# Reloading the second MLP's weights into whichever slot is freed next, with four staging slots and another rhythm of weight conversion

## The chip, the cores and the metric

One core of a Trainium2 chip runs the whole kernel in one launch. The metric is device time in microseconds (us). The kernel before took 1173.22 us, the median of three runs from 1171.08 to 1174.09. Its engines are TensorE (PE, with its weight loads as PEld), VectorE (DVE), ScalarE (ACT), GpSimd (POOL) and SyncE (SP), which issues every DMA of the part looked at here.

## The reference

Attention with a learned bias is followed by two MLPs; the change lies in the second one.

```python
x = attention(q, k, v, bias)              # 2304 tokens x 512
h = x @ w_in; x = (h - tanh(h)) @ w_out   # first MLP, 2048 wide
gate = 1 / (1 + exp(-(x @ w_gate)))       # second MLP, 1536 wide
out = (gate * (x @ w_val)) @ w_out2
```

All data are float32. Each matrix operand is split into a high and a low part (fp32r), and each product is three matmuls: high by high, low by high, high by low.

## The kernel before

**Units and slots.** The second MLP works on 18 units, listed in `PAIRS`. A unit is one pair of 384-token blocks (768 tokens) with one pair of 128-wide feature tiles, `fp`, of six. The list goes through five segments (`SEGS`): tokens 0 with `fp` 0 to 2, tokens 1 with `fp` 0 to 2, tokens 2 with all six, then tokens 0 and 1 again with `fp` 3 to 5. Units are numbered from 0 here. Tokens change after units 2, 5, 11 and 14, and this is what "a change of tokens" means below. A unit takes 14 slots (`slot2`), numbered 0 to 13: seven combined products `j` (a Strassen-like scheme with seven products in place of eight) for the gate half (`m` = 0, slots 0 to 6) and the same seven for the value half (`m` = 1, slots 7 to 13). Over the whole stage slot s is slot s mod 14 of unit s // 14.

**A slot.** It issues six matmuls of a product into one of two PSUM banks (`product`, L866), then, in twelve of the 14 slots, three matmuls of the second projection of the unit before (`down`, L882; slots 12 and 13 have none). Then the bank is emptied (`evacuate`: ACT at L924 and L931, DVE at L927, L933, L937, L941). The two banks alternate, so the product of a slot waits until the product two slots earlier has been emptied. POOL multiplies by the gate (L952) and makes low parts (L916), ACT makes high parts (L701).

**Weights.** Each unit needs nine weight tiles of 512 KB: seven for the products, in the order of their slots, and two for the second projection. They are converted once, stored in DRAM (`wsc`, L609), and reloaded for each unit that uses them (`feed`, L815), 162 reloads in all. Before, the reload with number k always takes place k mod 13 of a ring of 13 SBUF slots, and so waits until the reload k - 13 has been used for the last time (`spent`). Three other slots are staging for newly converted tiles on their way to DRAM (`W.stages`).

**Conversion.** Some weights are still converted while the second MLP runs (`convert`, advanced by one step after a slot). A weight item takes DVE operations at L547, L548, L549 and L545, ACT casts at L556, POOL operations at L554 (low part) and L604 (mix) and an ACT scan at L533. It runs through seven steps before, so one item in seven slots, from slot 8 of the stage to about slot 123. No step is taken in slots for which `slot2` returns true.

**Change of tokens.** In the last unit of a segment, in slots 7 to 13, `x_next` makes the next tokens' operands: for each product ACT casts two tiles (L797), POOL and DVE subtract one each (L797), and DVE does two more operations at L792. In the slots around it the old token results leave (L893 and L896 on DVE and ACT, L898 on SP) and new tokens are read (L775).

The order of the work on each engine is the order in which the code is written; there is no scheduler. Each engine's queue is taken in order, SP's too.

Of the kernel before, what the change touches and what calls it, by code (L numbers as in the profile page):

```python
# [436 lines left out]
GROUPS2 = len(PRODUCTS)  # L437
SLOTS2 = 2 * GROUPS2
PER_FP = GROUPS2 + 2
X_SLOTS, T_SLOTS, RING_SLOTS = tuple(range(14)), (14, 15), 13  # L440
STAGE1 = (0, 1, 2, 3)
X0_AT = N1 - 4
SEGS = ((0, 0, 3), (1, 0, 3), (2, 0, NFP), (0, 3, NFP), (1, 3, NFP))
# [191 lines left out]
def mlps(tc, st, xr, x0, W, xs, x2s, y2s, out, consts):  # L635
# [137 lines left out]
    def src_load(tau, kt):  # L773
        sx[kt] = x0.tile([128, TP], F32, name="xt")
        nc.sync.dma_start(sx[kt], x2s[128 * kt:128 * kt + 128, TP * tau:TP * tau + TP])  # L775
# [26 lines left out]
          N1: ([], [(4, 0), (4, 1)])}  # L802

    loads = [(u, i) for u in range(len(PAIRS)) for i in range(PER_FP)]
    ring, held, issued, spent = [], {}, [0], set()

    def feed():
        while issued[0] < len(loads):
            k = issued[0]
            u, i = loads[k]  # L810
            fp = PAIRS[u][2]
            if (fp, i) not in W.stored or k >= len(ring) and (k < RING_SLOTS or loads[k - RING_SLOTS] not in spent):
                return
            w = W.slot(ring[k % RING_SLOTS])
            nc.sync.dma_start(w.bitcast(F32).rearrange("p a c -> p (a c)"), W.wsc[fp][i])  # L815
            held[loads[k]] = w
            issued[0] += 1

    freed = {W.of[k, f]: LAST[1, f // NPR] + (3 if k == "o" else 1) for k in "io" for f in range(FA, NF1)}
    RING = sorted(freed, key=lambda i: (freed[i], i))  # L820

    def convert():
        while W.made <= W.n:
            highs, lows, mixes, conv = W.step()
            for f in conv[:2]:
                f()
                yield
            for f in highs + lows:
                f()
            for f in conv[2:]:  # L830
                f()
                yield
            for f in mixes:
                f()
            yield
            W.scan()
            yield
            yield
    banks, sums, posts, downs, res = [], [], {}, [], {}

    def at(s, f):
        posts.setdefault(s, []).append(f)
# [9 lines left out]
    def mat(s):  # L852
        g, j = divmod(s, GROUPS2)
        u, m = divmod(g, 2)
        return u, m, j

    def product(s):
        u, m, j = mat(s)
        w = held[u, j]
        p = banks[s % 2]  # L860
        fresh = j in (0, 1, 4)
        for kp in range(2):
            x = xw[PRODUCTS[j], kp]
            for i, (a, c) in enumerate(P3):
                o = 256 * m + 128 * kp
                T.matmul(p, w[:, a, o:o + 128], x[:, c], start=(fresh and kp == 0 and i == 0),  # L866
                         stop=(kp == 1 and i == 2), skip_group_check=True)
        if m:
            spent.add((u, j))

    def down():
        if not downs:
            return
        u, f, t, d, last = downs.pop(0)
        g, tau, fp, at_, n = PAIRS[u]
        h, l = res[u, f, t]
        w = held[u, GROUPS2 + f]
        begin = at_ == 0 and f == t
        end = at_ == n - 1 and f != t
        c = slice(128 * d, 128 * d + 128)  # L880
        for i, (x, a) in enumerate(((h, 0), (h, 1), (l, 0))):
            T.matmul(sums[3 * t + d], x[:, c], w[:, a], start=(begin and i == 0), stop=(end and i == 2))  # L882
        if last:
            spent.add((u, GROUPS2 + f))
        if end:
            return lambda: leave(g, t, d)

    def leave(g, t, d):
        tau, lo, hi = SEGS[g]
        r = TB * t + 128 * d  # L890
        if lo:
            o = kept.pop((t, d))
            V.tensor_add(o, sums[3 * t + d], o)  # L893
        else:
            o = ob.tile([128, DM], F32, name="o")
            (V.tensor_copy if d % 2 else A.copy)(o, sums[3 * t + d])  # L896
        r += TP * tau
        nc.sync.dma_start((out if hi == NFP else y2s)[r:r + 128, :], o)  # L898
# [66 lines left out]
    def slot2(s):  # L965
        u, m, j = mat(s)
        g, tau, fp, p, n = PAIRS[u]
        W.tick()
        feed()
        product(s)  # L970
        left = down()
        evacuate(s)
        if left:
            at(s + 1, left)
        for f in posts.pop(s, []):
            f()
        if g + 1 < len(SEGS):
            if p == n - 3 and m == 1 and j < 4:
                src_load(SEGS[g + 1][0], j)
            if p == n - 2 and j < 3:  # L980
                combine(m, j)
            if p == n - 1 and m == 1:
                x_next(j)
        if SEGS[g][1] and p == n - 1 and m == 0 and j < 6:
            bring(tau, j)
        return g + 1 < len(SEGS) and (p == n - 2 and j < 3 or p == n - 1 and m == 1 and j == 2)

    def x_next(j):
        k = PRODUCTS[j]
        for kp in range(2):  # L990
            for f in x_make(k, kp, (G, V)[kp]):
                f()
        if k == 2:
            for kp in range(2):
                combine(kp, 3)
# [4 lines left out]
    s = 0  # L1000
    for n in range(N1 + 3):
        if n < N1:
            W.tick()
        if n == 2:
            acc = st.enter_context(tc.tile_pool(name="ps_a", bufs=4, space=PSUM, side="right"))
        acts = second(n - 1) if ok(n - 1) else []
        acts[2:2] = [lambda m=m: fourth(m) for m in due(n, 1)]
        vecs = [f for m in due(n, 0) for f in third(m)]
        low, mixes, conv = [], [], []
        if 2 <= n < N1 and n not in X0_STEPS and not any(ends(m) and block(m)[2] for m in due(n - 1, 2)):  # L1010
            h, low, mixes, conv = W.step()
            acts += h
        if n in X0:
            conv = [lambda p=p: combine(*p) for p in X0[n][0]]
        for f in acts:
            f()
        zip_run(vecs, conv)
        if n in X0:
            for p in X0[n][1]:
                h, l = x_make(*p, G)  # L1020
                h()
                low.append(l)
        if n == N1:
            only1.close()
            ev = st.enter_context(tc.tile_pool(name="p3e", bufs=6))
            upst.close()
            one = st.enter_context(tc.tile_pool(name="ps_w", bufs=1, space=PSUM))
            banks = [one.tile([128, 512], F32, name=f"sum{i}")[:, 0:TB] for i in range(2)]
            W.raw2 = st.enter_context(tc.tile_pool(name="wr2", bufs=2))
            ob2 = st.enter_context(tc.tile_pool(name="p2o2", bufs=2))  # L1030
            W.stages = RING[RING_SLOTS:]
            W.lag = 4
        for _ in range({N1: 2, N1 + 1: 5}.get(n, 0)):
            slot2(s)
            s += 1
        for m in due(n - 1, 2):
            if ends(m):
                sixth(m)
        if ok(n):
            for _ in first(n):  # L1040
                if n < 2:
                    yield
        for m in due(n, 2):
            fifth(m)
        for l in low + mixes:
            l()
        if n < N1:
            W.scan()
        if ok(n) and ok(n + 1):
            for ahead in range(1, 5):  # L1050
                if ok(n + ahead) and block(n + ahead - 1) != block(n + ahead):
                    for f, lead in ((x_split, 3), (x_load, 4)):
                        for kt in range(4):
                            if lead - kt // 2 == ahead:
                                f(block(n + ahead), kt)
        if ok(n - 1) and block(n - 1)[2] == 1 and ends(n - 1):
            partial(n - 1)
        if n == X0_AT:
            for kt in range(4):
                src_load(0, kt)  # L1060
        if n >= X0_AT:
            ring += [i for i in RING if freed[i] == n or n == X0_AT and freed[i] < n]
            ring[RING_SLOTS:] = []
            feed()
        yield
    b = odd.tile([128, 2, 512], F32, name="up")
    sums = [b[:, i] for i in range(2)] + [acc.tile([128, 512], F32, name="acc") for _ in range(4)]
    conv = convert()
    while s < SLOTS2 * len(PAIRS):
        full = slot2(s)  # L1070
        if s == SLOTS2 // 2:
            for _ in range(2):
                W.load()
        if s > SLOTS2 // 2 and not full:
            next(conv, None)
        s += 1
        yield
# [124 lines left out]
```

## Time and profile before

| | |
|---|---|
| median of three runs | 1173.22 us (1171.08 to 1174.09) |
| profiled execution, its own time | 1171.4 us |
| span of its instructions | 1169.6 us |
| before the part of the second MLP alone, 0 to 738.67 us | PE busy 706.82 us |
| second MLP alone, 738.67 to 1169.60 us | PE busy 416.04 of 430.93 us, DVE 205.52, ACT 136.82, POOL 214.81 |
| weight reloads `w<-wsc` | 162 of 512 KB, median 7.4 us from issue to landing |

A share of busy time is an average over the stretch that it is taken from. An idle time in brackets in a timeline row is the time in which the engine stood still just before the row's first instruction, with what ended it.

### The profile page before, as it was taken

To read this page: it belongs to the slowest core of one execution; us is meant where nothing else is said; L and a number is where in the kernel's file an instruction comes from. 1 tells how busy PE (TensorE), PEld (TensorE's weight loads), DVE (VectorE), ACT (ScalarE), POOL (GpSimd) and SP (SyncE) were. 2 spreads that over 40 slices of the span, in tenths; PEclk is the share of its full clock that TensorE was granted. 3 is DMA by queue.
4 is the path that set the end of the run, shared out by engine and by line. 5 is a ranking of instruction groups with operands and counts; after the bars stand their busy time and mean duration, and the time that the engine had idled before them with its cause. 6 is when DMAs were issued, how large, how long until landed. Compare 5 with 4: busy or idle time off the path is not lost.

```text
span 1169.6 us, 19994 instructions
## 1 busy us (share of the span) xinstructions
PE 1122.9 (96%) x6968; PEld 978.5 (84%) x6968; DVE 829.3 (71%) x1443; ACT 672.6 (58%) x1341; POOL 667.9 (57%) x602
## 2 busy tenths in 40 slices
PE   5679999999999999999999999999989999999998
PEld 2246776677679999999999999998879999989987
DVE  8878888888659889898889887556566523533523
ACT  7877878787657676677766667234244222423321
POOL 1047777778635555496858667455676543523532
PEclk9889999999999999999999999999999999999999
DMA  6754636373213333355665667876987875685563
GB/s 202 258 177 129 195 112 199 121 210 108 86 48 103 105 107 114 127 195 182 213 207 176 214 238 266 292 274 243 353 313 286 310 294 210 247 295 219 220 255 138
DMA packets 107636, 235.09 MB, mean 201 GB/s; under 512 B 12688, under 2 KB 52880, under 8 KB 107536
## 3 DMA queue, kind: packets, MB, share of 16 engines
q1 hardware_dynamic: 107536, 233.82, 57.7%
q8 instruction: 56, 0.92, 0.3%
q14 instruction: 44, 0.36, 0.1%
HBM read 172.55 MB, written 61.22 MB: 200 GB/s over the span
## 4 chain that ended last, share of the span: by engine, by line
PE 86%; DMA 3%; ACT 3%; DVE 2%; issue 2%; POOL 2%; SPq 0%; DVEq 0%; ACTq 0%; POOLq 0%
PE sum L866 20%; PE acc L727 16%; PE up L663 16%; PE acc L882 8%; PE sc L227 6%; PE pv L319 6%; PE pt L269 6%; PE up L882 4%; DMA w<-wsc 2%; PE bt L75 1%; PE pv L316 1%; ACT e L86 1%; ACT y L62 1%; DMA bsc<-e 1%; POOL w L554 1%
## 5 line engine op out<-in xcount | busy, mean ns | idle before, releaser
L866 PE MATMUL sum<-w,w 128*128 128x384 f32 x1512 | 304.2, 340 | 10.4 <-DMA w<-wsc 3.3
L866 PEld LDWEIGHTS sum<-w,w 128*128 128x128 f32 x1512 | 270.2, 188 | 35.5 <-issue 5.8
L663 PE MATMUL up<-xt,w 128*128 128x384 f32 x1152 | 208.4, 335 | 0.3 <-DVE t L697 0.3
L663 PEld LDWEIGHTS up<-xt,w 128*128 128x128 f32 x1152 | 200.1, 188 | 2.9 <-issue 2.2
L727 PE MATMUL acc<-gh,w 128*128 128x384 f32 x768 | 195.5, 335 | 0.1
L259 POOL TENSOR_SCALAR n<-n,rec 128x576 f32<-128x576 f32 x144 | 120.8, 853 | 83.4 <-ACT n L248 41.1
L554 POOL TENSOR_TENSOR w<-wu,w 128x512 fp32r<-128x512 f32 x86 | 128.4, 1504 | 64.5 <-ACT w L556 64.5
L708 POOL TENSOR_TENSOR gl<-t,gh 128x384 fp32r<-128x384 f32 x96 | 103.8, 1103 | 91.2 <-issue 51.1
L727 PEld LDWEIGHTS acc<-gh,w 128*128 128x128 f32 x768 | 138.3, 188 | 1.2 <-DVE o L746 1.1
L727 PE MATMUL acc<-gl,w 128*128 128x384 f32 x384 | 128.3, 334 | 0.0
L241 DVE CUSTOM_DVE_ANT_0 n<-sc,bias 128x576 f32<-128x576 f32 x144 | 103.7, 753 | 29.7 <-PE sc L227 25.8
L916 POOL TENSOR_TENSOR gl<-e,gh 128x384 fp32r<-128x384 f32 x54 | 58.7, 1092 | 101.7 <-ACT gh L701 101.7
L248 ACT ACTIVATE n<-n,mn 128x576 f32<-128x576 f32 x144 | 111.4, 783 | 8.7 <-DVE mn L241 8.6
L701 ACT CAST gh<-t 128x384 fp32r<-128x384 f32 x114 | 57.7, 516 | 60.4 <-POOL t L952 59.3
L692 ACT ACTIVATE z<-z,c 128x768 f32<-128x768 f32 x48 | 45.2, 941 | 78.9 <-DVE up L691 78.8
L882 PE MATMUL acc<-w,gh 128*128 128x512 f32 x288 | 90.1, 393 | 0.0
L693 DVE TENSOR_TENSOR t<-up,t 128x768 f32<-128x768 f32 x48 | 46.0, 958 | 53.4 <-ACT t L680 52.7
L269 PE MATMUL pt<-ident,n 128*128 128x128 f32 x576 | 80.4, 281 | 1.4 <-ACT at L299 1.3
L654 POOL TENSOR_TENSOR xt<-xm,xt 128x384 fp32r<-128x384 f32 x48 | 49.3, 1047 | 53.9 <-ACT xt L653 50.5
L319 PE MATMUL pv<-at,vs 128*64 128x320 f32 (+1 forms) x512 | 79.3, 421 | 0.0
L941 DVE TENSOR_TENSOR e<-sum,e 128x384 f32<-128x384 f32 x70 | 38.8, 555 | 52.0 <-PE sum L866 52.0
L269 PEld LDWEIGHTS pt<-ident,n 128*128 128x128 f32 x576 | 63.5, 141 | 12.6 <-issue 11.4
(111 smaller groups left out, 2145.5 us busy)
## 6 DMA issues: line engine op xcount, KB each, us to landing
w<-wsc SPq DMA_DIRECT2D x162, 512.0 KB, 7.4
wsc<-w SPq DMA_DIRECT2D x54, 512.0 KB, 5.6
wraw<-in_wo SPq DMA_DIRECT2D x28, 512.0 KB, 4.4
bsc<-e SPq DMA_DIRECT2D x36, 295.5 KB, 3.1
xm<-xs SPq DMA_DIRECT2D x48, 192.0 KB, 3.2
x2s<-o SPq DMA_DIRECT2D x48, 192.0 KB, 3.7
wraw<-in_wi SPq DMA_DIRECT2D x16, 512.0 KB, 4.3
xt<-x2s SPq DMA_DIRECT2D x20, 384.0 KB, 6.8
```

What stands on the lines that cost most here:

```text
L227: T.matmul(sc[u, t][:, hf, 0:288], q[r, 128 * s:128 * s + 128], k[r, o:o + 288], start=(i == 0), stop=(i == 2))
L241: V.tensor_tensor_reduce(n.rearrange("p (a b) -> p a b", a=2), s[:, :, 0:288], bias[t].rearrange("p (a b) -> p a b", a=2), -0.125, 3.0e38, ...
L248: A.activation(n, n, AF.Exp, bias=m, scale=-1.0, accum_out=nsum[u, t // 4][:, t % 4:t % 4 + 1])
L259: G.tensor_scalar(n, n, nrec[u, t // 4][:, t % 4:t % 4 + 1], 1.0, ALU.mult, ALU.mult)
L269: T.transpose(pt[:, i], n[:, o:o + 128], ident)
L319: T.matmul(p[0][64 * a:64 * a + 64, 0:N], v[:, c - 1, a], main[:, c - 1, a * N:a * N + N], start=False, stop=(c == 4))
L554: self.nc.gpsimd.tensor_sub(w[:, 1], x, w[:, 0].bitcast(F32))
L663: T.matmul(p[:, 0:TB], w[:, a, 128 * kt:128 * kt + 128], x[:, c], start=(kt == 0 and i == 0), stop=(kt == 3 and i == 2))
L708: G.tensor_sub(l, x[:, j], h.bitcast(F32))
L727: T.matmul(ac[blk][d][:, 0:TB], w[:, a, 128 * d:128 * d + 128], c, start=(begin and j == 0 and i == 0), stop=(end and j == NPR - 1 and i = ...
L866: T.matmul(p, w[:, a, o:o + 128], x[:, c], start=(fresh and kp == 0 and i == 0), stop=(kp == 1 and i == 2), skip_group_check=True)
L882: T.matmul(sums[3 * t + d], x[:, c], w[:, a], start=(begin and i == 0), stop=(end and i == 2))
```

## The change

There are four edits. The fixed ring becomes a list of free slots: `spend` puts a slot on the list when its tile has been used for the last time, and `feed` takes the first slot of the list for the next reload, whichever tile lay in it. The reloads keep their order. The ring has 12 slots in place of 13, and the staging has four in place of three. A conversion item takes six steps in place of seven. And in the last unit of a segment no conversion step is taken in slots 7 to 13, where before only slot 9 was left out; the six slots in the unit ahead of it stay without conversion as before.

```diff
-X_SLOTS, T_SLOTS, RING_SLOTS = tuple(range(14)), (14, 15), 13
+X_SLOTS, T_SLOTS, RING_SLOTS = tuple(range(14)), (14, 15), 12
-    ring, held, issued, spent = [], {}, [0], set()
+    free, held, issued = [], {}, [0]
+
+    def spend(key):
+        free.append(held[key][0])
     def feed():
-        while issued[0] < len(loads):
-            k = issued[0]
-            u, i = loads[k]
+        while issued[0] < len(loads) and free:
+            u, i = loads[issued[0]]
             fp = PAIRS[u][2]
-            if (fp, i) not in W.stored or k >= len(ring) and (k < RING_SLOTS or loads[k - RING_SLOTS] not in spent):
+            if (fp, i) not in W.stored:
                 return
-            w = W.slot(ring[k % RING_SLOTS])
+            k = free.pop(0)
+            w = W.slot(k)
             nc.sync.dma_start(w.bitcast(F32).rearrange("p a c -> p (a c)"), W.wsc[fp][i])
-            held[loads[k]] = w
+            held[u, i] = k, w
             issued[0] += 1
...
             W.scan()
             yield
-            yield
...
         if m:
-            spent.add((u, j))
+            spend((u, j))
...
         if last:
-            spent.add((u, GROUPS2 + f))
+            spend((u, GROUPS2 + f))
...
-        return g + 1 < len(SEGS) and (p == n - 2 and j < 3 or p == n - 1 and m == 1 and j == 2)
+        return g + 1 < len(SEGS) and (p == n - 2 and j < 3 or p == n - 1 and m == 1)
...
-            ring += [i for i in RING if freed[i] == n or n == X0_AT and freed[i] < n]
-            ring[RING_SLOTS:] = []
+            free += [i for i in RING[:RING_SLOTS] if freed[i] == n or n == X0_AT and freed[i] < n]
```

**SP, the end of unit 3.** The names are w16 and so on for the SBUF slot and wsc1_2 for product 2 of `fp` 1 (numbers 7 and 8 are the second projection); y2s is the token output, xt the new tokens. Before:

```order
L898 DMA y2s_64<-o_9946 128x512
L815 DMA w25_9950<-wsc1_2_76 128x1024
L815 DMA w16_9952<-wsc1_3_77 128x1024
L815 DMA w18_9954<-wsc1_4_78 128x1024
L815 DMA w20_9956<-wsc1_5_79 128x1024
L815 DMA w22_9958<-wsc1_6_80 128x1024
L815 DMA w17_9960<-wsc1_7_81 128x1024
L815 DMA w19_9962<-wsc1_8_82 128x1024
L898 DMA y2s_64<-o_9972 128x512
```

Now the same loads stand from slot 8 of the unit on, between the outputs and the token reads:

```order
L818 DMA w22_9866<-wsc1_1_75 128x1024
L900 DMA y2s_64<-o_9880 128x512
L775 DMA xt_9883<-x2s_63 128x768
L609 DMA wsc4_0_101<-w25_9803 128x1024
L818 DMA w24_9888<-wsc1_2_76 128x1024
L818 DMA w20_9890<-wsc1_3_77 128x1024
L900 DMA y2s_64<-o_9903 128x512
L775 DMA xt_9906<-x2s_63 128x768
L516 DMA wraw_9911<-in_wg 128x2x256
L516 DMA wraw_9911<-in_wv 128x2x256
L818 DMA w23_9914<-wsc1_4_78 128x1024
L900 DMA y2s_64<-o_9930 128x512
```

The seven loads that stood in one piece behind five outputs are spread. So it is with the loads for units 2 to 17: those of products 2 to 6 stood at slot 12 of the unit ahead; now they stand at its slots 9, 9, 10, 11 and 12. The load of product 1 has moved from slot 0 to slot 8 of that unit, that of product 0 from the slot before it to slot 0.

**DVE, the first change of tokens (slots 9 to 13 of unit 2).** L797 and L792 make new operands, L937 and L941 empty banks, L549 and L545 convert a weight. Before:

```order
L792 TENSOR_TENSOR xt<-xt,w_9409 128x384
L937 TENSOR_TENSOR t<-sum_9038,e 128x384
L797 TENSOR_TENSOR w_9682<-xt,w_9682 128x384
L549 SCALAR_TENSOR_TENSOR wu<-wraw,wu 128x512
L941 TENSOR_TENSOR t<-sum_9039,t 128x384
L797 TENSOR_TENSOR w_9700<-w_9409,w_9700 128x384
L545 SCALAR_TENSOR_TENSOR wu<-wraw,wu 128x512
L941 TENSOR_TENSOR e<-sum_9038,e 128x384
L797 TENSOR_TENSOR w_9729<-xt,w_9729 128x384
L941 TENSOR_TENSOR e<-sum_9039,e 128x384
L797 TENSOR_TENSOR w_9748<-xt,w_9748 128x384
```

Now (L939 and L943 are the same operations as L937 and L941 before):

```order
L792 TENSOR_TENSOR xt<-xt,w_9408 128x384
L939 TENSOR_TENSOR t<-sum_9038,e 128x384
L797 TENSOR_TENSOR w_9689<-xt,w_9689 128x384
L943 TENSOR_TENSOR t<-sum_9039,t 128x384
L797 TENSOR_TENSOR w_9708<-w_9408,w_9708 128x384
L943 TENSOR_TENSOR e<-sum_9038,e 128x384
L797 TENSOR_TENSOR w_9726<-xt,w_9726 128x384
L943 TENSOR_TENSOR e<-sum_9039,e 128x384
L797 TENSOR_TENSOR w_9745<-xt,w_9745 128x384
L545 SCALAR_TENSOR_TENSOR wu<-wraw,wu 128x512
```

L549 has moved ahead of the first L797 of the unit, L545 behind the last; L547 and L548 of the same item, which stood between the first three L797, have moved ahead too.

**POOL, the second change of tokens (unit 5).** L554 makes low parts of converted weights, L797 new operands, L952 the product with the gate, L916 the low part of a result. Before:

```order
L797 TENSOR_TENSOR w_10382<-xt,w_10382 128x384
L554 TENSOR_TENSOR w_10327<-wu,w_10327 128x512
L554 TENSOR_TENSOR w_10328<-wu,w_10328 128x512
L916 TENSOR_TENSOR gl<-e,gh 128x384
L797 TENSOR_TENSOR w_10404<-w_10011,w_10404 128x384
L952 TENSOR_TENSOR t<-t 128x384
L797 TENSOR_TENSOR w_10433<-xt,w_10433 128x384
L952 TENSOR_TENSOR e<-e 128x384
L797 TENSOR_TENSOR w_10452<-xt,w_10452 128x384
```

Now (L918 and L954 are L916 and L952 of before):

```order
L797 TENSOR_TENSOR w_10388<-xt,w_10388 128x384
L918 TENSOR_TENSOR gl<-e,gh 128x384
L797 TENSOR_TENSOR w_10407<-w_10005,w_10407 128x384
L954 TENSOR_TENSOR t<-t 128x384
L797 TENSOR_TENSOR w_10425<-xt,w_10425 128x384
L954 TENSOR_TENSOR e<-e 128x384
L797 TENSOR_TENSOR w_10444<-xt,w_10444 128x384
L918 TENSOR_TENSOR gl<-t,gh 128x384
L954 TENSOR_TENSOR e<-e 128x384
L554 TENSOR_TENSOR w_10294<-wu,w_10294 128x512
L554 TENSOR_TENSOR w_10295<-wu,w_10295 128x512
```

The two L554 have moved from the middle of the operands into slot 0 of the next unit.

## Rows read from the trace of the kernel before

**Rows 1.** The page: the span, and section 4, the chain by engine.
```profile
span 1169.6 us, 19994 instructions
PE 86%; DMA 3%; ACT 3%; DVE 2%; issue 2%; POOL 2%; SPq 0%; DVEq 0%; ACTq 0%; POOLq 0%
```

**Rows 2.** Busy time by stretch: the second MLP alone (columns in the first row).
```profile
core 0: us, PE busy (x) PEld busy (x) DVE busy (x) ACT busy (x) POOL busy (x), PEclk, DMA share, GB/s
738.67:1169.60 430.93, 416.04 (x2119) 380.14 (x2118) 205.52 (x329) 136.82 (x281) 214.81 (x188) 1.00 0.70 265
```

**Rows 3.** Busy time by stretch: the same six slots at token changes 1, 3 and 2.
```profile
786.52:800.55 14.03, 11.22 (x49) 9.42 (x48) 12.92 (x19) 7.20 (x16) 11.41 (x10) 0.88 0.63 240
1006.83:1016.34 9.51, 9.49 (x50) 8.50 (x49) 8.98 (x15) 6.40 (x14) 8.47 (x8) 1.00 0.32 109
862.77:876.06 13.29, 9.93 (x49) 8.21 (x48) 12.64 (x18) 5.55 (x13) 10.68 (x9) 1.00 0.65 239
```

**Rows 4.** Timeline of PE, first change (start, length, instruction, count, idle before).
```profile
792.00 1.31 PE L866 MATMUL sum<-w,w 128*128 128x384 f32 x6
794.72 1.32 PE L866 MATMUL sum<-w,w 128*128 128x384 f32 x6 [1.40 <-DVE t L941]
797.45 2.26 PE L866 MATMUL sum<-w,w 128*128 128x384 f32 x6 [1.41 <-ACT w L797]
```

**Rows 5.** Timeline of DVE, first change.
```profile
792.70 1.50 DVE L549 SCALAR_TENSOR_TENSOR wu<-wraw,wu 128x512 int32<-128x512 int32 x1
794.12 0.55 DVE L941 TENSOR_TENSOR t<-sum,t 128x384 f32<-128x384 f32 x1
...
795.39 1.49 DVE L545 SCALAR_TENSOR_TENSOR wu<-wraw,wu 128x512 int32<-128x512 int32 x1
796.80 0.54 DVE L941 TENSOR_TENSOR e<-sum,e 128x384 f32<-128x384 f32 x1
```

**Rows 6.** Timeline of POOL, second change.
```profile
868.58 3.27 POOL L554 TENSOR_TENSOR w<-wu,w 128x512 fp32r<-128x512 f32 x2
```

**Rows 7.** Timeline of ACT, second change.
```profile
875.86 0.52 ACT L701 CAST gh<-t 128x384 fp32r<-128x384 f32 x1 [5.41 <-POOL t L952]
```

**Rows 8.** Timeline of PE at the three waits for reloads, and two undisturbed slots.
```profile
824.17 1.22 PE L866 MATMUL sum<-w,w 128*128 128x384 f32 x6
...
827.20 1.28 PE L866 MATMUL sum<-w,w 128*128 128x384 f32 x6 [1.11 <-DMA w<-wsc]
...
974.83 1.22 PE L866 MATMUL sum<-w,w 128*128 128x384 f32 x6
...
976.59 1.22 PE L866 MATMUL sum<-w,w 128*128 128x384 f32 x6
...
1043.04 1.28 PE L866 MATMUL sum<-w,w 128*128 128x384 f32 x6 [1.59 <-DMA w<-wsc]
...
1117.40 1.30 PE L866 MATMUL sum<-w,w 128*128 128x384 f32 x6 [0.62 <-DMA w<-wsc]
```

**Rows 9.** Timeline of SP: the reloads at the end of unit 3.
```profile
821.02 4.47 SPq L815 DMA_DIRECT2D w<-wsc  x7
```

**Rows 10.** Line L815: all reloads from issue to landing.
```profile
DMA to landing us min/median/max: 3.6/7.4/11.5
```

**Rows 11.** Waits of SP's queue from 680 us on (sum, times, longest).
```profile
SPq L815 <- PE acc L882: 131.7, 12, 18.3
...
SPq L898 <- DVE o L893: 37.5, 11, 19.1
```

**Rows 12.** Busy time by stretch: conversion with no change of tokens, slots 98 to 120.
```profile
898.26:937.39 39.13, 39.13 (x202) 36.10 (x202) 19.84 (x30) 13.57 (x28) 25.14 (x22) 1.00 0.87 327
```

**Rows 13.** Timeline of ACT within that stretch, and line L549 over the whole trace.
```profile
934.82 0.62 ACT L556 CAST w<-wu 128x512 fp32r<-128x512 f32 x1 [7.70 <-DMA wsc<-w]
...
L549 DVE SCALAR_TENSOR_TENSOR wu<-wraw,wu x68: 676/910/1765, 72.1 to 928.4; 128x512 int32<-128x512 int32 x68
```

**Rows 14.** Timeline of PE, slot 0 of unit 1.
```profile
746.51 1.34 PE L866 MATMUL sum<-w,w 128*128 128x384 f32 x6 [0.33 <-DVE e L941]
```

More of the change, by code (lines that the diff above doesn't have):

```diff
@@ L858, in product @@
         u, m, j = mat(s)
-        w = held[u, j]
+        w = held[u, j][1]
         p = banks[s % 2]
@@ L876, in down @@
         h, l = res[u, f, t]
-        w = held[u, GROUPS2 + f]
+        w = held[u, GROUPS2 + f][1]
         begin = at_ == 0 and f == t
@@ L1069, in mlps @@
     while s < SLOTS2 * len(PAIRS):
-        full = slot2(s)
+        crowded = slot2(s)
         if s == SLOTS2 // 2:
@@ L1073, in mlps @@
                 W.load()
-        if s > SLOTS2 // 2 and not full:
+        if s > SLOTS2 // 2 and not crowded:
             next(conv, None)
```

## The prediction

> **What bounds the kernel now.** I read the page first: the chain that ended last is PE for 86% of a span of 1169.6 us [rows 1], so a microsecond counts where PE stands still or runs slowly. Then busy time by stretch: in the second MLP, the only part that the change touches, PE is busy for 416.04 of 430.93 us, while DVE, ACT and POOL have 205.52, 136.82 and 214.81 us of work [rows 2]. So only 14.9 us are idle, and some of that is the end of the kernel, after the last matmul. What the change can give is in this idle time and in the clock, and the question is at which slots it lies. The timeline of PE shows two kinds of place.
>
> The first is a change of tokens while weights are still converted. The second compares directly with one that has no conversion: the same six slots, from slot 9 of the last unit to the start of slot 1 of the next, take 14.03 us at change 1, 13.29 us at change 2, and 9.51 us at change 3, with the same matmuls [rows 3]. Conversion is over by change 3. At change 1 two products wait 1.40 and 1.41 us [rows 4]. The rows of DVE say for what: L549 runs 1.50 us and the bank is emptied by L941 only behind it, at 794.12 to 794.67, and the waiting product starts at 794.72; L545 runs 1.49 us, L941 follows at 796.80 to 797.34, and the next product starts at 797.45 [rows 4, 5]. The row of PE names an ACT cast for the second wait, but that cast belongs to other operands; the bank fits to a tenth. DVE was busy for 12.92 of the 14.03 us, against 8.98 of 9.51 at change 3 [rows 3]. The granted clock averages 0.88 there, so PE ran part of it at the lower level, 1.2 GHz; 12% of 14.03 us below full, at half rate, is 1.7 us lost after the waits. 2.81 of waits and 1.7 of clock make 4.5, which is the difference to change 3.
>
> The second kind is a reload that lands late. Three products wait for `w<-wsc`: 1.11, 1.59 and 0.62 us [rows 8]. They are products 2, 2 and 4 of units 4, 13 and 16. In the first, the loads are issued in one piece of seven from 821.02 us [rows 9], for a product that could have started about 1.76 us after 824.17 (the step of undisturbed slots, 976.59 less 974.83) and started at 827.20 [rows 8].
>
> **The change part by part.** *Conversion out of the change of tokens.* DVE loses four operations (L547, L548, L549, L545) between slots 7 and 13, POOL at change 2 also two L554, 3.27 us [rows 6], which stood before the gate product that ACT waited 5.41 us for [rows 7]. What is left is the work of change 3, which shows what is late next: nothing by more than 0.02 us of PE idle in 9.51 [rows 3]. So change 1 gives 14.03 - 9.51 = 4.52 us and change 2 gives 13.29 - 9.51 = 3.78 us, 8.30 together. Changes 3 and 4 have no conversion to lose: 0. Where POOL's two L554 go, slot 0 of the next unit, POOL's next results are wanted at slot 3 or later, so I put their cost at 0; without that cover it would be their 3.27 us.
>
> *Reloads in the order of freed slots.* A product's load used to stand at slot 12 of the unit ahead; product 2 had four slots of lead and shared the queue with six other loads. Now the shortest lead is seven slots, for products 1 and 2. Seven slots are about 7/6 of 9.51, 11.1 us, against a median landing of 7.4 us that itself comes from loads issued in one piece; the quickest took 3.6 [rows 3, 10]. The three waits go. Idle time was 3.32 us; from start to start the first cost 3.03 - 1.76 = 1.27, so 0.16 more than its idle time [rows 8]. Three times that is about 0.5: 3.8 us. No reload is added, 162 before and after, and one slot fewer in the ring costs nothing while the lead is seven slots.
>
> *Four staging slots.* They end waits of ACT on the store of a staged tile, up to 7.70 us [rows 13]. That one lies in a stretch in which PE was busy for 39.13 of 39.13 us [rows 12]: ACT's wait was covered by free PSUM banks, so 0.
>
> *Six steps in place of seven.* The same DVE, ACT and POOL operations fall on fewer slots. In slots 98 to 120, where an item took seven slots and no tokens changed, PE never stopped and DVE was busy for 19.84 of 39.13 us [rows 12]. One sixth denser adds at most 3.3 us of DVE work to that stretch, far under its 19.3 free. Four DVE operations still stand in consecutive slots, as before; only which slots they meet is new. The bounds: from a gain of about 1 us, the small stalls at unit starts that could go (one is 0.33 us [rows 14]), to a loss of the whole 8.3 us, if the stall moves with the operations. I take 0, by the nearest row, that stretch.
>
> A rule of the Trainium skill speaks against this part. What the rows show: L549 takes 0.676 us at its quickest and 1.50 us at the change, beside POOL's L797 and L916 [rows 5, 13]. SBUF - State Buffer, section Who interferes with whom, says that a DVE instruction with two SBUF inputs and a GpSimd instruction that reads SBUF cannot run together, and the one that comes second waits out the first. The length agrees with it. By that rule alone the moved operations meet POOL's work elsewhere and lengthen there too; by it the time is that of the rival "the stall moves", 1169.4 us, and by the stretch without a wait 1159.3.
>
> **The sum.** 4.52 + 3.78 + 3.8 = 12.1 us. The profiled execution took 1171.4 us (span 1169.6 and 1.8 around it), so 1159.3. It lies 1.8 under the median of the runs, 1173.22; from that median the time is 1161.1. I predict 1161 us.
>
> **The rivals.** *The stall moves.* The eight DVE operations, and POOL's beside them, stand in front of a bank somewhere else, and PE waits there. For it: an operation of 1.5 us and 0.55 of emptying make 2.05, more than a slot of 1.76, so four in a row run 1.2 us late at worst [rows 5, 8]. Against it: [rows 12], where the same four in a row cost nothing. Of the sum 3.8 us remain: 1169.4 us.
>
> *The reload waits stay.* If the loads are late because SP is behind outputs, moving them ahead in the code moves nothing; only 8.3 us go: 1165 us. For it: the piece of seven stands right behind five outputs of tokens in the order. Against it: SP issued all seven within 4.47 us as soon as it came to them, and its long wait there was for PE's last use [rows 9, 11], which is what the change loosens.
>
> *Slower: a load behind a waiting output.* Before, SP waited for PE once per unit, 131.7 us in 12 waits, and for outputs up to 19.1 us [rows 11]; all loads then went at once. Now six or seven loads of each unit stand each behind its own wait, with outputs, token reads, stores and conversion reads between them, and whatever waits holds the load behind it. The point where it decides is issue plus landing beyond the lead of 11.1 us; the longest landing seen is 11.5 [rows 10]. One microsecond late in each of 16 units costs 16 us; with only the 8.3 us of the changes of tokens gained, 7.7 us slower: 1181 us; it turns slower than before from half a microsecond. Against it: the waits shown are SP's free time, since nothing was due behind them, and spread loads do not stand behind six others on the DMA engines.
>
> On that point the Trainium skill says, in DMA: Bandwidth & Descriptors, section Anatomy of one DMA - SWDGE (gpsimd) path, that DMA engines do not wait on semaphores, so that a wait holds the issuing engine. The waits of SP's queue agree [rows 11]. By it a load is as late as the wait ahead of it, the 1181 us of this rival; without it a load would be as early as its place in the code, the 1159.3 of the sum.
>
> *No effect.* Both kinds of wait are replaced by equal ones: 1173 us. The order on SP, DVE and POOL shows that the instructions did move, so this needs two new waits.
>
> **How the numbers follow.** The forecast, a gain of 9.5 to 13 us, 0.66; the stall moves, 0.15; the reload waits stay, 0.08; no effect, 0.05; slower, 0.06. A measurement of this kernel can tell 0.3%, 3.5 us, from no change. The stall that moves gives 3.8 us, just over that, so I split it, 0.10 faster and 0.05 same. Faster: 0.66 + 0.08 + 0.10 = 0.84; same: 0.05 + 0.05 = 0.10; slower 0.06. The low end is the forecast less the 1 us of small stalls and the 2 us by which the runs of before differ from their median: 1158. The high end reaches to the stall that moves, 1169.5. The forecast's own range is 1158 to 1164.
>
> **What would show it.** Right: six slots at changes 1 and 2 in about 9.5 us at a granted clock of 1.00, no wait of PE for `w<-wsc`, PE busy for all but about 5 us of the second MLP, which is then about 419 us long. Wrong: PE waits for a bank emptied behind L549 or L545 in units with no change of tokens; PE waits for products 1 or 2 at the start of units; SP waiting on outputs while a load behind is due; or a granted clock under 1.00 at a new place.

## The result and the profile after

The changed kernel takes 1160.02 us, the median of six runs from 1157.07 to 1162.49, against 1173.36 us (1169.21 to 1175.54) before: a ratio of 0.9892, 95% interval 0.9869 to 0.9915, or 12.7 us faster with an interval from 10.0 to 15.4. The forecast was 1161 us, with 1158 to 1164 as its own range.

The profiled execution took 1161.68 us. Busy time by stretch, of the kernel after: the second MLP from its first slots on (columns: length, PE, PEld, DVE, ACT and POOL busy with instruction counts, granted clock, DMA share, GB/s), then the six slots at changes of tokens 1, 2 and 3, which answer to [rows 2, 3].

```profile
739.64:1159.90 420.26, 413.19 (x2119) 379.57 (x2118) 212.02 (x329) 138.39 (x281) 216.82 (x188) 1.00 0.74 273
787.49:796.98 9.49, 9.49 (x49) 8.49 (x48) 8.96 (x15) 6.38 (x14) 8.45 (x8) 1.00 0.97 333
860.12:869.62 9.50, 9.49 (x49) 8.49 (x48) 8.97 (x15) 6.39 (x14) 8.46 (x8) 1.00 0.97 333
999.70:1009.22 9.52, 9.50 (x50) 8.50 (x49) 9.00 (x15) 6.41 (x14) 8.49 (x8) 1.00 0.93 317
```

The stage is 430.93 - 420.26 = 10.7 us shorter. Changes 1 and 2 took 14.03 and 13.29 us and now cost what change 3 costs, with DVE 4 us less busy and the clock at 1.00. The span fell by 9.7 us only, 1169.6 to 1159.9; the stage began 1.0 us later in this execution (739.64 for 738.67), in a part that the change does not touch. Of the kernel after, the waits of PE from 738 us on (sum, times, longest):

```profile
PE sum L868 <- DMA w<-wsc: 1.9, 2, 1.0
PE sum L868 <- DVE e L943: 0.3, 1, 0.3
PE sum L868 <- ACT e L926: 0.2, 1, 0.2
PE up L884 <- POOL gl L918: 0.2, 1, 0.2
```

The waits behind DVE at the changes are gone, and so are the three waits for reloads of [rows 8]; but two new ones stand for a reload. The timeline of PE, kernel after, shows them in unit 4, at products 4 and 5:

```profile
826.80 1.28 PE L868 MATMUL sum<-w,w 128*128 128x384 f32 x6 [1.04 <-DMA w<-wsc]
...
829.65 1.30 PE L868 MATMUL sum<-w,w 128*128 128x384 f32 x6 [0.88 <-DMA w<-wsc]
```

What was issued ahead of these reloads, in the timeline of SP, kernel after (L900 is a token output, L775 a token read, L609 the store of a converted tile, L516 a read of raw weights, L818 a reload):

```profile
810.11 0.32 SPq L900 DMA_DIRECT2D y2s<-o  x1
810.52 0.38 SPq L775 DMA_DIRECT2D xt<-x2s  x1
811.00 0.40 SPq L818 DMA_DIRECT2D w<-wsc  x1
811.84 0.32 SPq L900 DMA_DIRECT2D y2s<-o  x1
812.22 0.42 SPq L775 DMA_DIRECT2D xt<-x2s  x1
812.73 0.43 SPq L609 DMA_DIRECT2D wsc<-w  x1
813.26 1.75 SPq L818 DMA_DIRECT2D w<-wsc  x2
815.10 1.04 SPq L900 DMA_DIRECT2D y2s<-o  x1
816.19 0.87 SPq L775 DMA_DIRECT2D xt<-x2s  x1
817.12 0.44 SPq L516 DMA_DIRECT2D wraw<-in_wg  x1
817.60 0.47 SPq L516 DMA_DIRECT2D wraw<-in_wv  x1
818.59 0.34 SPq L818 DMA_DIRECT2D w<-wsc  x1
819.85 0.34 SPq L900 DMA_DIRECT2D y2s<-o  x1
821.04 0.32 SPq L775 DMA_DIRECT2D xt<-x2s  x1
822.38 0.32 SPq L818 DMA_DIRECT2D w<-wsc  x1
```

The reload of product 4 goes out at 818.59, that of product 5 at 822.38, about 6 and 8 us after the slots in which they stand, 10 and 11 of unit 3, whose products start at 812.8 and 814.6 us. They land at 826.67 and 829.52 us, each 0.13 us before its product starts. What SP waits for, in the waits of its queue from 800 to 832 us:

```profile
SPq L900 <- ACT o L898: 10.1, 1, 10.1
SPq L818 <- DMA w<-wsc: 1.8, 2, 1.0
SPq L818 <- DMA xt<-x2s: 1.0, 2, 0.6
```

The long wait, for a token output, ends at 810.11, ahead of all the rows above. The waits of the reloads behind it are short, and most of that time is for the landing of earlier transfers. All reloads of the kernel after land faster than before, 6.6 us in the median against 7.4 [rows 10], which fits that they no longer go out in one piece:

```profile
DMA to landing us min/median/max: 3.2/6.6/9.6
```

### The profile page after: what moved, and what is told of

Its sections match the earlier page's. It is cut to its first block, busy times and chain, and to the rows that moved or that the text cites. A ratio compares the mean times of both kernels' runs of the same rounds, so it can differ in the third digit from the quotient of the medians.

```text
span 1159.9 us, 20092 instructions
## 1 busy us (share of the span) xinstructions
PE 1120.7 (97%) x6968; PEld 977.5 (84%) x6968; DVE 832.5 (72%) x1443; ACT 674.0 (58%) x1341; POOL 669.6 (58%) x602
## 4 chain that ended last, share of the span: by engine, by line
PE 87%; DMA 3%; ACT 3%; DVE 3%; issue 2%; POOL 1%; SPq 0%; DVEq 0%; ACTq 0%; POOLq 0%
PE sum L868 22%; PE acc L727 17%; PE up L663 16%; PE acc L884 8%; PE sc L227 6%; PE pv L319 6%; PE pt L269 5%; PE up L884 4%; DMA w<-wsc 1%; DMA bsc<-e 1%; PE pv L316 1%; PE bt L75 1%; DVE y L64 1%; ACT e L86 1%; ACT y L62 1%
## 5 line engine op out<-in xcount | busy, mean ns | idle before, releaser
L554 POOL TENSOR_TENSOR w<-wu,w 128x512 fp32r<-128x512 f32 x86 | 127.9, 1498 | 30.4 <-ACT w L556 30.4
L918 POOL TENSOR_TENSOR gl<-e,gh 128x384 fp32r<-128x384 f32 x54 | 58.0, 1081 | 117.3 <-ACT gh L701 117.3
L943 DVE TENSOR_TENSOR e<-sum,e 128x384 f32<-128x384 f32 x70 | 38.8, 555 | 48.7 <-PE sum L868 48.6
```

Source lines behind the costliest of these rows:

```text
L554: self.nc.gpsimd.tensor_sub(w[:, 1], x, w[:, 0].bitcast(F32))
```

## The experiments

Two questions were open: does each half of the gain belong to its own edit, and what holds up the reloads of unit 4? The kernel before was timed beside each; its medians there are 1171.63, 1171.67 and 1171.46 us.

**Only the reloads and the staging.** The changed kernel with the old rhythm of conversion:

```diff
             W.scan()
             yield
+            yield
...
-        return g + 1 < len(SEGS) and (p == n - 2 and j < 3 or p == n - 1 and m == 1)
+        return g + 1 < len(SEGS) and (p == n - 2 and j < 3 or p == n - 1 and m == 1 and j == 2)
```

> Only the reloads by freed slot and the four staging slots; conversion in its old rhythm, also during a change of tokens. Theory (two separate gains): the six slots at changes 1 and 2 still take about 14.0 and 13.3 us, the waits for reloads at units 13 and 16 are gone, that at unit 4 is gone or replaced by up to 2.4 us; time 1169 to 1171.5 us, ratio to before 0.997 to 0.9985. Rival (the four staging slots or the spread reloads freed ACT and SP and so ended the stalls at the changes): both stretches about 9.5 us, time near 1161 us.

1169.42 us, ratio 0.998 (0.9965 to 0.9996). The six slots at changes 1 and 2, busy time by stretch of this kernel:

```profile
784.93:799.19 14.26, 11.45 (x50) 9.60 (x49) 12.91 (x19) 7.33 (x16) 11.64 (x10) 0.88 0.94 334
861.05:875.86 14.81, 11.49 (x50) 9.63 (x48) 13.01 (x19) 7.09 (x16) 12.20 (x10) 0.83 0.95 343
```

The changes stay slow, so staging and reloads did not end those stalls. At change 2 the granted clock now falls too, to 0.83 on average, though the waits of PE there are those of before (1.64 and 1.68 us against 1.67 and 1.69); this takes back part of what the reloads gave. Two waits for reloads, 0.60 us in unit 4 and 0.32 us in unit 13, remain out of 3.3; the second was expected to be gone.

**Only the conversion rules.** The kernel before with six steps and the pause:

```diff
             W.scan()
             yield
-            yield
...
-        return g + 1 < len(SEGS) and (p == n - 2 and j < 3 or p == n - 1 and m == 1 and j == 2)
+        return g + 1 < len(SEGS) and (p == n - 2 and j < 3 or p == n - 1 and m == 1)
```

> Only the conversion rules (six steps, none in slots 7 to 13 of the last unit of a segment); the ring of 13 slots and three staging slots as before. Theory: the six slots at changes 1 and 2 take 9.5 us each at a granted clock of 1.00, the waits for reloads stay at 3 to 4 us; time about 1164.5 us, ratio 0.9925. Rival (staging and reloads end the stalls): changes stay at 13 to 14 us, time over 1170 us.

1169.41 us, ratio 0.9981 (0.9966 to 0.9996): 5 us more than expected, though the changes take 9.51 and 9.49 us. Two new stalls ate the gain. The timeline of PE of this kernel shows them in units 4 and 8:

```profile
822.38 2.26 PE L865 MATMUL sum<-w,w 128*128 128x384 f32 x6 [3.74 <-DMA w<-wsc]
...
932.73 1.51 PE L865 MATMUL sum<-w,w 128*128 128x384 f32 x6 [2.15 <-ACT e L923]
```

The length of the first, 2.26 us for six matmuls in place of 1.22, is the lower clock behind the wait. The second is ACT's lateness, in its timeline of the same kernel:

```profile
927.89 0.62 ACT L556 CAST w<-wu 128x512 fp32r<-128x512 f32 x1 [7.47 <-DMA wsc<-w]
```

The cast waits 7.47 us for the store that frees its staging slot, and the bank emptied at L923, at 932.21 us, stands behind it. ACT waits once more in between, 1.40 us for POOL at L604, so this run does not show how much of the 2.15 us is the store's. Before, such a wait of 7.70 us was free [rows 12, 13].

**Only the pause.** The second line of the diff above alone, with seven steps.

> Only the pause: no conversion step in slots 7 to 13 of the last unit of a segment; seven steps, the old ring and staging. Theory: the pause alone makes the changes 9.5 us each, time as with both conversion rules within 1.5 us, about 1164.5 us. Rival (the six steps matter, since they bring the items to other slots): the changes stay over 11 us, or waits of over 2 us stand elsewhere.

1163.37 us, ratio 0.9925 (0.9905 to 0.9945). The six slots at changes 1 and 2:

```profile
785.21:794.70 9.49, 9.47 (x49) 8.48 (x48) 8.97 (x15) 6.39 (x14) 8.45 (x8) 1.00 0.46 179
856.41:865.90 9.49, 9.47 (x49) 8.48 (x48) 8.97 (x15) 6.39 (x14) 8.45 (x8) 1.00 0.35 121
```

The pause alone makes the larger part of the gain, as expected. PE still waits 4.5 us for reloads in this kernel, in three waits, of which two are:

```profile
820.81 1.30 PE L866 MATMUL sum<-w,w 128*128 128x384 f32 x6 [0.99 <-DMA w<-wsc]
...
892.98 1.28 PE L866 MATMUL sum<-w,w 128*128 128x384 f32 x6 [1.96 <-DMA w<-wsc]
```

Against the run before it, six steps cost 6 us on the old ring and staging.

**Seven steps in the changed kernel.** The first `yield` put back, the rest as changed.

```diff
             W.scan()
             yield
+            yield
```

> The changed kernel with seven steps for an item in place of six. Theory: the changes stay at 9.5 us; in unit 3 the store of a converted tile moves from slot 8 to slot 12, behind the reloads that were late, so the 1.9 us of waits at unit 4 shrink by a half or more; time 1158 to 1160 us. Rival (six steps are needed, the old rhythm costs bank waits): over 2 us of waits for a bank, time over 1162 us. Second rival (the waits at unit 4 come from SP standing behind outputs, not from traffic): they stay at about 1.9 us.

1156.9 us (1155.88 to 1157.41), ratio 0.9867 (0.9845 to 0.989); no wait for a reload is left. The waits of PE from 738 us on:

```profile
PE sum L869 <- DVE e L944: 0.3, 1, 0.3
PE sum L869 <- ACT e L927: 0.2, 1, 0.2
PE up L885 <- POOL gl L919: 0.2, 1, 0.2
```

In the timeline of SP of this kernel the store stands behind the reloads, and the reload of product 4 goes out at 813.50, where with six steps it stood behind the store and two reads of raw weights until 818.59 (this execution runs 1.45 us ahead there: its unit 1 starts at 746.00 in place of 747.45):

```profile
811.23 1.00 SPq L818 DMA_DIRECT2D w<-wsc  x2
...
813.50 0.57 SPq L818 DMA_DIRECT2D w<-wsc  x1
...
821.56 0.32 SPq L609 DMA_DIRECT2D wsc<-w  x1
```

**The changed kernel again,** beside the three that follow.

> The changed kernel once more, for a comparison on the same chip with the three below. Both theories: 1158 to 1162 us, waits of PE for reloads only at unit 4, products 4 and 5, about 1.9 us of idle time.

1159.38 us (1158.34 to 1159.78), ratio 0.9896 (0.9877 to 0.9915); the same two waits, 0.71 and 0.88 us.

**Token reads early.**

```diff
-            if p == n - 3 and m == 1 and j < 4:
+            if p == n - 3 and m == (g == 0) and j < 4:
```

> The changed kernel with the four token reads of a segment moved from slots 7 to 10 to slots 0 to 3 of the same unit (not in unit 0), where SP was idle. Theory (the reloads of unit 4 are late by the DMA traffic that stands ahead of them, 1.5 MB of it token reads, with no more than eight DMAs in flight): the waits at unit 4 go, 2 to 2.4 us faster than the changed kernel, about 1158 us. Rival (SP stands behind an output that waits for ACT until 810 us): the output still waits, the waits stay at 1 us or more.

1156.15 us (1155.34 to 1156.88), ratio 0.9868 (0.9847 to 0.989): 3.2 us under the changed kernel beside it, where 2 to 2.4 were expected, and all its runs lie under all runs of that one. No wait for a reload is left among the waits of PE from 738 us on:

```profile
PE sum L868 <- DVE e L943: 0.3, 1, 0.3
PE sum L868 <- ACT e L926: 0.2, 1, 0.2
PE up L884 <- POOL gl L918: 0.2, 1, 0.2
```

**Output bytes early.**

```diff
-        nc.sync.dma_start((out if hi == NFP else y2s)[r:r + 128, :], o)
+        c = slice(0, DM if hi == NFP else 64)
+        nc.sync.dma_start((out if hi == NFP else y2s)[r:r + 128, c], o[:, c])
...
+        if g in (1, 2) and p == 0 and m == 0 and j < 6:
+            r = TP * SEGS[g - 1][0] + 128 * j
+            nc.sync.dma_start(y2s[r:r + 128, 64:DM], sx[0][:, 0:DM - 64])
```

> The changed kernel in which the token outputs of units 3 and 6 write 64 of 512 columns at their old place, with their old waits, and the other 448 columns are written (with other values, so the result is another) in slots 0 to 5. The bytes and the order at the end of the unit are those of the changed kernel but for 1.4 MB moved forward. Theory (traffic): the reloads come earlier by up to 1.4 MB at 400 GB/s, 3.4 us, so the 1.9 us of waits at unit 4 go; time 2 us under the changed kernel. Rival (SP waits for outputs in order): the outputs wait as before, the waits at unit 4 stay at 1.5 us or more.

1158.16 us (1157.04 to 1158.82), ratio 0.9884 (0.9863 to 0.9906). The outputs keep their places and their waits (SP stands 8.6 us for the first one, until 809.53), yet no wait for a reload is left. The waits of PE from 738 us on, then the rows that answer to the SP timeline above:

```profile
PE sum L868 <- DVE e L944: 0.3, 1, 0.3
PE sum L868 <- ACT e L927: 0.2, 1, 0.2
PE up L884 <- POOL gl L919: 0.2, 1, 0.2
```

```profile
809.53 0.32 SPq L901 DMA_DIRECT2D y2s<-o  x1
...
816.79 0.35 SPq L818 DMA_DIRECT2D w<-wsc  x1
...
820.62 0.32 SPq L818 DMA_DIRECT2D w<-wsc  x1
```

From the first output to the reload of product 4 it is 7.26 us here and 8.48 in the changed kernel (818.59 - 810.11); to that of product 5 11.09 and 12.27. So waiting outputs in SP's order do not by themselves make PE wait, and fewer bytes ahead are enough to end the waits. Outputs that do not wait, with all their bytes, were not tried. In medians the gain is 1.2 us, less than the 2 expected, and the two sets of runs overlap; in the traces, from the first product of unit 1 to the end, it is 2.0 us (410.14 against 412.13).

**Ten reload slots.**

```diff
-X_SLOTS, T_SLOTS, RING_SLOTS = tuple(range(14)), (14, 15), 12
+X_SLOTS, T_SLOTS, RING_SLOTS = tuple(range(14)), (14, 15), 10
...
-            W.stages = RING[RING_SLOTS:]
+            W.stages = RING[12:]
```

> The changed kernel with 10 reload slots in place of 12 (four staging slots, two slots unused): the loads of products 0 to 5 of a unit stand five to six slots ahead of their use in place of seven to fourteen. It asks from which lead the slower rival decides. Theory: a load alone lands in 3.2 to 4 us, and five slots are 7 to 9 us, so in units without token outputs PE still does not wait; in the units after a change of tokens (4, 7, 13, 16) waits of 2 to 6 us each; time 1166 to 1178 us. Rival (a load waits out more than its own landing everywhere): a wait in nearly each of 16 units, over 1180 us.

1168.36 us, ratio 0.9975 (0.996 to 0.9989). PE's waits for reloads are 6.3 us in seven, all in units 1, 4 and 13. Units 7 and 16, where waits were expected too, have none: the units ahead of them, 6 and 15, have outputs but no token reads, while units 3 and 12 have both. Unit 0, ahead of unit 1, has token reads and conversion, and there the one wait is 0.38 us. The longest is in the timeline of PE at slot 0 of unit 4, with a lower clock behind it:

```profile
819.10 2.01 PE L868 MATMUL sum<-w,w 128*128 128x384 f32 x6 [2.65 <-DMA w<-wsc]
```

A lead of five to six slots is enough where reloads meet outputs alone; in the changed kernel seven to eight are not where outputs, token reads and conversion meet.

**Three staging slots,** with six steps as below, and with seven (there the `yield` is put back too):

```diff
-            W.stages = RING[RING_SLOTS:]
+            W.stages = RING[13:]
```

> The changed kernel with three staging slots (the fourth is left unused); 12 reload slots and six steps as in the changed kernel. Theory (six steps bring a staging slot back before its store has landed, ACT stands for it and a bank is emptied late): ACT waits 7 us or more for a store near slot 119 and PE 2 us or more there, with a drop of the granted clock behind it possible: 2 to 4 us slower than the changed kernel, 1162 to 1164 us. Rival (the staging slots cost nothing, and the wait in the run with the conversion rules alone came from its old ring): no wait of PE near slot 121, 1159 to 1160 us.

> The changed kernel with three staging slots and seven steps. Theory: seven steps leave the stores time, so three staging slots cost less than 0.5 us, as in the kernel before; no wait of PE over 0.4 us anywhere past unit 1; 1156 to 1158 us, as with four staging slots and seven steps. Rival (three staging slots are short at any rhythm): 2 us or more of waits near the end of the conversion, over 1159 us.

Six steps: 1160.87 us, ratio 0.9916 (0.9894 to 0.9938), 1.5 us over the changed kernel's 1159.38 (ratio 0.9896, the intervals overlap) and less than the 2 to 4 expected. The wait is there, but in unit 4 and not near slot 121. In the timelines of ACT and PE:

```profile
834.77 0.62 ACT L556 CAST w<-wu 128x512 fp32r<-128x512 f32 x1 [4.85 <-DMA wsc<-w]
```

```profile
835.82 1.31 PE L868 MATMUL sum<-w,w 128*128 128x384 f32 x6 [1.47 <-ACT e L926]
```

Seven steps: 1157.56 us, ratio 0.9886 (0.9864 to 0.9907), and ACT waits for a store 0.2 us in all:

```profile
ACT w L556 <- DMA wsc<-w: 0.2, 1, 0.2
```

**Both,** early token reads and seven steps.

> The changed kernel with token reads in slots 0 to 3 of the unit and with seven steps. Theory: both remove the same waits at unit 4, so together they give no more than either: 1155.5 to 1157.5 us, no wait of PE for a reload. Rival (each removes a part of its own): 2 us under the better of the two, below 1154.5 us.

1157.03 us (1156.64 to 1158.28), ratio 0.9885 (0.9864 to 0.9907): no better than either, as expected. Token reads early, 1156.15 us, and seven steps, 1156.9 us, are the fastest versions run; between them these runs do not decide.

## Why the prediction was right, and where it was not

*Conversion out of the changes of tokens:* 4.52 + 3.78 = 8.30 us were forecast; measured 14.03 - 9.49 = 4.54 and 13.29 - 9.50 = 3.79, 8.33 us. Both figures start from the same 14.03 and 13.29 us of one execution, so what was tested is that the two changes would come down to change 3's 9.51 us, and they did. The run with the pause alone ties it to that edit. The price itself depends on where the clock falls: with the reloads alone the two changes took 14.26 and 14.81 us, 10.05 us over twice change 3.

*Reloads:* the three waits went, as forecast. The step that failed is that seven slots of lead hold everywhere. In unit 4 two new waits came, 1.04 + 0.88 = 1.92 us of idle time in place of 3.32, so 1.4 us of it went, where the term of 3.8 us counted on all. The load of product 4 has eight slots of lead in the code, from 812.82 to 825.76 us, but it went out 5.8 us after its slot began and took 8.1 us to land. Issue plus landing beyond the lead is the slower rival's own condition; it was met at one unit and not at 16. An output that waits was not enough for that, as the output run shows. In its slot SP had six other transfers to issue first, in 0.43 to 1.04 us each, and then waited 0.5 us for a landing; ahead of the load of product 5 it waited for landings three times. A wait for the landing of other transfers is what the prediction had not listed. From 818 to 844 us the kernel after moves 403 GB/s, and 369 or less in each of the other stretches of 26 us between 740 and 1130; there the outputs of a segment, the next token reads and conversion have met.

*Six steps:* put at 0 from a stretch without a change of tokens. That no bank is emptied late by the denser conversion held, with four staging slots; "the stall moves" did not come, and nor did the loss that I had drawn from the Trainium skill (SBUF — State Buffer, Who interferes with whom). By that rule an operation of DVE with two SBUF inputs waits out one of GpSimd that reads SBUF and started first; the lengths agree, 0.676 and 1.50 us [rows 5, 13]. The operations did lengthen: from 740 us on, L549 takes 1.30 us in the median in the kernel after and 0.89 before. Yet PE's longest wait for DVE there is 0.3 us, so the lengthening cost it nothing that shows. The steps also carry DMAs, though. They put a store and two reads of raw weights ahead of unit 4's reloads, and cost 1160.02 or 1159.38 against 1156.9 us, some 2.5 to 3 us; in the traces, from the first product of unit 1 to the end, 412.42 against 409.63, 2.8 us. I had weighed the edit on the engines and not on the queue.

*Four staging slots:* put at 0, and that holds at seven steps (1157.56 against 1156.9 us, ratios 0.9886 and 0.9867 with overlapping intervals). At six steps the fourth slot is worth 1.47 us of PE's idle time. So in these runs it pays only for what the six steps bring.

*The sum:* 12.1 us forecast, 12.7 (10.0 to 15.4) measured; in the trace the stage lost 10.7 us. That the two lie so close is in part luck. From the first product of unit 1 to the end, the traces show 423.09 us before and 409.63 with seven steps: the other edits give 13.5 us, 1.4 more than forecast, and six steps take back 2.8, which were put at 0. Of the signs named beforehand the first came, 9.49 and 9.50 us at a clock of 1.00; the second did not, with two waits for reloads; and PE was idle for 7.07 us of 420.26, where about 5 of 419 were expected.

One reading of the rows was loose: SP's 12 long waits for PE [rows 11] are not one in each of the 18 units.

That only unit 4 waits fits the traffic: unit 3 ahead of it has outputs, token reads and conversion, unit 12 has no conversion, units 6 and 15 have no token reads. It is near the edge without conversion too: with the reloads alone, unit 13 waited 0.32 us. Which share of the traffic is enough was not measured; moving any one of three, the store with its raw reads, the token reads or the output bytes, took the waits away.

## What to carry to other kernels

Where a stretch repeats with and without a suspected load, the difference of the two is the price of that load, clock included; here the stretch came down to within 0.02 us of the one without. The price holds for the execution that it was read from. When background work is moved, follow its DMAs through the queue as well as its operations through the engines, above all past transfers with a deadline. A wait that costs nothing is only covered: a wait of ACT of 7.70 us cost PE nothing before, and one of 7.47 us stood ahead of a 2.15 us wait of PE in the run with the conversion rules alone.

## What the runs showed of the hardware

The order of issue on SP was not held up by waiting outputs alone: in the trace of the changed kernel none of the 665 DMAs was issued before the eighth DMA ahead of it had landed, and 41 were issued within 0.12 us of that landing; in the kernel before it was the same, with 48. Every one of these DMAs tells of its landing by the semaphore that the eighth ahead of it used, one of eight taken in turn. So this program keeps at most eight DMAs in flight, and once they are the large ones at the end of unit 3, each next reload goes out at the pace at which they land. That shows as short waits of SP for a transfer that has nothing to do with its own, and as rows of SP a good microsecond apart between 818.59 and 822.38. Whether more than eight in flight would help was not tried.

The drop of the granted clock came behind some waits of PE and not behind others: at change 1 before it averaged 0.88 with waits of 1.40 and 1.41 us, at change 2 it stayed at 1.00 with 1.67 and 1.69 us, and the run with the reloads alone had 0.83 there with 1.64 and 1.68. For nearly the same waits that stretch took 13.29 us in the one execution and 14.81 in the other, so the fall of the clock was worth some 1.5 us within it. Each is one execution; what decides between the two is not shown.
